# Up projections 512 tokens wide and a seven-product down projection in three banks, in a fused attention and feed-forward kernel

## The chip, the core and the metric

The kernel runs on one core of one Trainium2 chip. The metric is the device time of one execution in microseconds (us). Five instruction queues work side by side: TensorE (PE in the profile, its weight loads PEld), VectorE (DVE), ScalarE (ACT), GpSimd (POOL) and SyncE (SP). They meet only at semaphores.

## What is computed

The reference has two parts. The first is attention with chunk selection, for 4 batches of 8 heads, 768 positions and 64 columns each:

```
ub = sum_d max(q * k_min, q * k_max)          # a bound per query and chunk of 32 keys
top_chunks = the 6 chunks of largest bound, among those not after the query
scores = q @ k.T / 8, kept where the chunk is chosen and the key is not after the query
x = softmax(scores) @ v                       # then [4 * 768, 8 * 64] = [3072, 512]
```

The second is a feed-forward layer over these 3072 tokens, with `w_in` of 512 x 2048 and `w_out` of 2048 x 512:

```
h = max(x @ w_in, 0)
out = (h * h) @ w_out                         # float32, 3072 x 512
```

The kernel takes float32 and multiplies in bf16.

## The kernel before

**Tiles and stages.** Tokens are handled in tiles of 128. The first tile of each batch attends only to itself; these four tiles go through the feed-forward layer together (`x_first`, lines 1401 to 1414). The other five tiles of each batch (640 tokens) follow batch by batch (loop of lines 1451 to 1487): attention writes `x`, `turn` gives its transpose `xT`, `up` makes `h`, and `down` or `down_pair` makes the output rows.

**`up` (line 1203).** One call takes one of 16 blocks of 128 columns of `w_in` and a run of tokens. Four matmuls (line 1214) sum over the 512 input columns in one PSUM bank (`ph`), a ReLU on ScalarE (line 1221) or VectorE (line 1223) writes `ht`, and a square on VectorE (line 413) or ScalarE (line 411) writes into `h2`, the tile that the profile calls `h`. In a batch, tiles 0 and 1 are one run (256 tokens) and tiles 2 to 4 another (384 tokens): two calls for each block (lines 1472 to 1477). An `h2` buffer holds two blocks for all tokens of the batch; there are ten (line 389).

**`down_pair` (line 1236), batches 1 to 3.** Two tiles t and t+1, two halves of the 2048 hidden columns and two halves of the 512 output columns make a 2 x 2 by 2 x 2 block product, done in seven products instead of eight. It needs four combinations of the weights, made once, and sums of blocks of `h`: S1 = upper + lower at t+1, S2 = S1 minus lower at t, S3 = lower at t minus lower at t+1, S4 = upper at t minus S2. Each is made in four pieces 256 elements wide (line 1252). Each product is two parts of four matmuls (line 1288), 256 columns wide, into one half of a PSUM bank:

```
bank 0: P1 | P2    bank 1: P6 | P5    bank 2: P7 | P4    bank 3: P3 | -
```

VectorE adds them up in the output tiles `ob` (`add_up`, line 1325): C11, U2, U4, C22, U3, C21 and C12, each 256 wide, after a copy of P1 to `ob` on either engine. Tile 4 of these batches, and all tiles of batch 0, use `down` (line 1369): four parts of four matmuls, 512 wide (line 1379), then a copy (line 405 or 407). The last batch's tile 4 is cut into 384 and 128 columns. The stores (line 1365) go out on SP, for batches 1 and 2 on POOL.

**What sets the order.** Every operation is entered in a `Plan` (lines 204 to 326) with the engines it may use. `SEQUENCE` (lines 46 to 157) is a written list of all operations by number with a letter for the engine. `Plan.order` gives each a planned start and buffer slots, sorts by start, and `write` issues them in that order on each engine, with matmuls on a constant tile as fillers ahead of early PE operations that are planned to wait (`keep_warm`). Banks in PSUM: three for scores and, in the last batch, the feed-forward layer (`ps`), two for it in the other batches (`ff`), two for the attention sums, one for transposes. The waits are derived from the written order: an operation that writes a bank waits for an operation before it in that order that reads it.

Of the kernel before, what the change touches and what calls it, by code (L numbers as in the profile page):

```python
# [9 lines left out]
F32 = mybir.dt.float32  # L10
# [36 lines left out]
4 61D 6 0 1 131 2 19 8 20 14A 12D 11A 26 5D 21 10D 134 23 135A 9D 22 18 146 7 24 3D  # L47
150 147A 17D 31 136 148 132 25 149D 133A 15D 151 27 176 152 137 177D 28 138 160 142 32
139 140 161A 141 156 33 153 143 174 154 178 155 29 175A 157 179 158 30 144 162 145 180
159 188 184 34 181 163D 190 189A 185 191D 13G 164 182 165 183 35 186 166 187 170 198  # L50
36 192 199D 41 167 171 193A 195 168 172 200A 169 48 196A 286 173 206 197A 194D 204 40
207D 205A 287 280 201 288 54 282A 211 202D 281A 39 212D 208 290D 214 209A 213D 283
215A 217 210A 47 223 284 218A 203A 44 226 219A 285 224A 216D 43 289D 291 227A 343 292
220 225A 293 345A 229 294 295 221A 38 344D 296 230A 232 222D 297A 42 347 235 298A 46
299A 346 313 233A 309 50 228D 314 349 300D 241 236A 45 351 350 310 317 348 301 51 237A
231D 354 234D 238 302 352D 242A 355 334 49 318 353D 250 356 335 62G 60 239A 412 357
322 16 305 251A 414 55 244 358 306 413 323 315G 359 307D 326 243D 247 416A 363D 303G
311D 324G 362D 327 304 52 308 248D 312 330 360A 316 338 331 53 319 253 361D 252D 339
56 415D 364 385 245D 365 368 332G 406 336G 240D 369 325 372 320 328G 256 410 373 370G
59 386 329 409 333 376 254A 380 69 389 377 337 387D 262 411 408D 67 381 321 397 407A  # L60
417 378G 366D 340 257 418 68 398 420 390 367 249D 469 374G 341 246A 401 419 37 393 371
471A 263 421 399G 391D 342 402 422 375 66 379 424D 394 382 388 423D 258 395G 426D 64
383 425A 472 439 435 392 396 436 400 403 470D 427 440 264 255D 428 473 71 431 448 432
259 404 384 65 449 429D 475 452 433G 477 456 73 453 265 437D 476 457 474 57 443 260D
478A 460 480 441D 261 430 70 444 450D 434 481 268 461 482 58 479A 464 483 438 442 445
484 269 72 465 405 266A 485 81 270 486D 462D 78 487D 451 731 488D 498 735 274 458G 499
454G 79 489A 490 446 500D 494 734 491 506 98 455 459 463 495 466 515 732D 271 83 516
733D 507 511 736 496G 467 502 272A 737 74 468 519 512 447 275 82 85 492D 503 738 493
520 739 527 523 513G 741D 497 501 521G 524 742 504D 517G 276 80 740A 743 77 525D 744
505 528 508 794 76 745 514 518 795A 509 522 746 526 529 114 277 530 510 796A 531 94  # L70
747 278A 749D 532 748D 104 533A 534 750D 760 535A 797 584 86 119 585A 539 798 761 764
75 542 540A 768 751D 765 800 541D 578 799 543A 766G 801 777 769 536 90 803D 579A 752
544D 537A 756 802 575 110 753 580D 572 804D 576A 805 762G 573A 577D 545 111 95 538D
757 557 806 546A 574D 857 754G 807 558A 548 758G 547A 87 559D 105 566 859A 549D 781
808 560 100 567A 809 858A 267 581 561D 99 568D 551 562D 782 861 773 582A 755 783G 810
552A 759 91 554 550D 774 812D 763 569 860 583A 775G 789 555A 128 84 767 811A 556D 863
570D 814A 563 862 813A 571D 586 89 867D 770 564A 785 865 587A 776 588 864 778 638 589D
786 779G 1022 88 790 868 96 565D 819 553D 590 866A 771 869 787G 815 820 273 591D 668
92 816 823 870 593 670A 817G 871 780 102 784 594D 831 669A 827 872 788 129 596 124
821D 828 671 639 832 829G 597A 672 836 873 595A 791 108 640 824 877D 598D 837 641 792  # L80
825G 592D 876A 117 673 1021 840 875A 605 874A 772 93 793 674 642A 894 676 878 841 599
675 606A 842D 818 879 106 886 600D 608 895 601D 838G 611 1177A 609D 880G 63G 844 125
607D 822 612A 1117 617 887 882 618A 826 678D 97 830 602 883 613D 610D 620 677A 120
1118 101 833 603A 848 881 884G 1300 621A 890 614 845 1301 622A 126 679 623 891 1176D
107 615A 885 892G 680 899 619A 1119 888G 626 681 900 846G 889 682 103 893 624A 896
901G 903 834 683 122 616A 852 644 835 627A 1179 904 839 121 843 632 625A 1237D 1303
849 684 645 1245D 633A 109 897 850G 1121 628A 1120 907 1302 629 1183A 1178 118 643 646
630A 127 685D 908 905G 1180 635 686D 604A 1304 909G 1124 898 130 688A 116 701 853 1125
647 1238D 687A 1182 1307 1126 702 847 851 689 1127 636A 902 703G 906 1239 697 690 693
650 698 1023 694 699G 911 1240 854 1184A 722 691G 718 695G 651 723 1128 1550 912 1129  # L90
855 910 714 1024 719 652 913G 1308 715 856 112 123 705 648A 710 1181 726 1571 631A 692
720G 696 1244D 700 1185 706 1116D 279 656 1572 711 724G 1309 637A 113 657 1122D 634A
1123D 1310 1132A 712G 914 704 716G 1186 653 1133A 1115D 727 1311 915 1131D 1130A 1167
1312 707 1188 1159 654A 658 708 1187 1160 709 655 659 1168 1161G 1189 916 1306D 1169G
1190 1134 1028 1305A 1138 713 717 1027 917 721 1139 725 728 1163 729 1135 662 918 730
1164 1136G 919 1146 1315A 1155 1547 1165G 920 1171 1140G 1147 663 1156 1316D 1148G
1549 1142 1172 921 1192D 1137 664 1191D 1143 1313D 1194A 1195 1546 1144G 1199 971 660A
115 1150 1141 1193A 1145 1149 1298D 665 1157G 1548 1151 1314D 970 1613 1200 1551 1203
666A 922 1552 1204 1207 972 1026 1152 925 923A 1205G 1612 1208 1158 1211 928 926A 661
1209G 1162 1196 1616 649 1166 1170 1615 1173 1201G 931 929A 1241 927D 924A 1216 1553  # L100
934 932A 1197G 1212 1554 940 1555 935A 1224 933D 1217 1153 937 930D 1614 941A 1228
936D 938A 1556 946 1225 1025 943 1557 947A 1226G 1232 939D 942A 1220 1299D 949 944A
1154 1218G 945A 952 948D 950A 1568 1617 953A 1198 955 1229 951D 1202 967 954A 956D
1230G 1558 1233 1317 1174 968D 964 1221 1175 1206 958 957D 965A 1222G 1618 1329 959A
961 1569 966A 1210 1213 969A 973 962A 1242 1029 960A 1219 976 1243 974A 1214 1040 963A
1619 979 1560 977A 975D 1561 1223 1034 985 980A 1620 1559 1318 1621 982 1562 1570 986A
981D 1573 1035 983A 978D 988 987D 1330 1574 991 989A 1036 1331G 1622 1246 992A 994
990D 1247 984A 1000 1038 995A 1248 993A 1003 1001D 996A 1037 1227 1006 1249 1004A 1250
1002A 1012 1576 1007A 1251 1032 1321 1005A 1593 1009 1030 1013A 1575 667 1010A 1015
1033 1008D 1577 1041 1016A 1578 1042 1011A 1031 997 1579 1591 1045A 1565 1014A 1043  # L110
1564 998A 1252D 1044 1253A 1039 1231 1567 1018 1046 1017A 1215 1566 1255A 1264 1319D
1268 1322 1254D 1047 1590 999A 1580 1048 1323G 1265 1623 1234 1053 1019D 1269 1256
1054 1055 1257 1050 1272 1074 1320 1057 1071 1273 1258G 1056 1285 1270G 1235 1324 1260
1049 1286 1058 1236 1261 1293 1266D 1287G 1061 1059 1583 1020D 1262G 1277 1584 1062
1259 1281 1278 1051 1060 1582 1294 1263 1267 1581 1063 1342 1271 1279D 1274 1343 1068
1075 1064 1052 1275 1289 1282 1338 1276 1344G 1081 1290 1283G 1592 1350 1072 1339 1280
1073 1082 1291D 1563 1069 1325 1284 1076 1065 1326 1078 1077 1083 1351 1066 1333 1327D
1288 1340G 1079 1292 1346 1070 1334 1354 1295 1067 1328 1347 1332 1296 1084 1297 1355
1335 1352G 1097 1348D 1085D 1341 1634 1336 1594 1086 1345 1644 1349 1337 1353 1356
1087 1638 1357 1088 1358 1635 1093 1080 1359 1095 1641 1094 1092 1091 1098 1090 1647  # L120
1089 1360 1096 1099 1642 1657 1645 1104 1648 1101 1410 1105 1636 1651 1100 1106 1654
1637 1102 1595 1107 1411 1643 1109 1103 1596 1108 1639 1361 1597 1660 1586 1362A 1598
1110 1585 1363A 1599 1674 1600 1588 1661 1640 1364 1675 1601 1652 1111 1365A 1662
1366A 1646 1409 1671 1370 1587 1653 1112 1371A 1672 1666 1658 1649 1367 1372A 1667
1602 1677 1368A 1113D 1650 1681 1373 1655 1114 1382 1369D 1678 1374D 1659 1668 1589
1383A 1656 1376 1669 1687 1375D 1379 1384D 1377A 1670 1663 1380A 1682 1424 1684 1378D
# [203 lines left out]
def kernel(  # L330
# [795 lines left out]
    sums = {}  # L1126
# [42 lines left out]
    def ffn(x, ready, rows, by_dma, due, rate, up_tags=("ff", "ff"), by_pool=False):  # L1169
# [33 lines left out]
        def up(f, c0, c1, i):  # L1203
# [4 lines left out]
            if f // 2 not in h2:  # L1208
                h2[f // 2] = buffer("h2", [128, 2, 128 * n])
# [241 lines left out]
    for b in range(B):  # L1451
# [68 lines left out]
```

## Time and profile before

| | us |
|---|---|
| median of 3 runs | 261.51 (261.18 to 262.19) |
| the profiled execution | 261.52 |
| its span in the profile | 259.8 |
| around the span | 1.7 |
| TensorE busy in the span | 245.2 |
| VectorE, ScalarE, GpSimd busy | 219.9, 200.6, 118.0 |

The profiled execution is as long as the median. Busy times are sums over one engine. A matmul row lasts longer than its distance to the next one, since matmuls are pipelined; so a busy TensorE may still issue less than it could, and the distances of starts tell more. `PEld` rows with idle time "issue" are weight loads that did not start although the engine's queue was in their place: the load or its matmul stood at a wait.

### The profile page before, as it was taken

Reading aid. Unit: us, or ns where it says so; the run is one execution under the profiler, and the core shown is the slowest. Engines: PE = TensorE matmul, PEld = TensorE weight load, DVE = VectorE, ACT = ScalarE, POOL = GpSimd, SP = SyncE. Lnnn points to the kernel's source line nnn. Section 1 sums busy time; section 2 is a strip of 40 time slices with the busy share of each in tenths; the row PEclk is TensorE's granted clock in tenths of the full one; section 3 lists DMA queues with packets and bytes.
Section 4 is the critical chain, followed back from the end, with each engine's and each line's share of the span. In section 5 each row is a group of like instructions: output and inputs, shape, how many; then the busy total and the mean of one; then the engine's idle time right before and its main releaser. Section 6 shows DMA issues by size and latency. Waiting matters only on the chain. (4 is left out here: it accounts for less than half of the span.)

```text
span 259.8 us, 7199 instructions
## 1 busy us (share of the span) xinstructions
PE 245.2 (94%) x2633; PEld 174.7 (67%) x2649; DVE 219.9 (85%) x780; ACT 200.6 (77%) x423; POOL 118.0 (45%) x202
## 2 busy tenths in 40 slices
PE   8779999999999999999999998999999999999993
PEld 5556466666687566556687676867776776867773
DVE  5559999989999999999999988888888994578752
ACT  6558999878999999899999896748988961883300
POOL 8999698999985935372411304222022210000000
PEclk9999999999999999999999999999999999999999
DMA  9999999999999999956736529453796025111112
GB/s 131 126 161 190 173 155 193 172 164 141 152 145 188 163 159 131 150 85 104 104 115 144 96 72 187 112 127 84 182 187 106 0 83 101 43 42 44 40 71 91
DMA packets 117283, 31.92 MB, mean 123 GB/s; under 512 B 99840, under 2 KB 114944, under 8 KB 117248
## 3 DMA queue, kind: packets, MB, share of 16 engines
q0 software_dynamic: 77968, 16.00, 72.2%
q1 hardware_dynamic: 39280, 15.47, 30.7%
q8 instruction: 20, 0.33, 0.5%
q14 instruction: 15, 0.12, 0.2%
HBM read 32.77 MB, written 6.55 MB: 151 GB/s over the span
## 5 line engine op out<-in xcount | busy, mean ns | idle before, releaser
L1214 PE MATMUL ph<-xT,w_in_sb 128*128 128x256 bf16 (+2 forms) x592 | 98.8, 304 | 1.1 <-ACT ht L1221 0.2
L1074 ACT ACTIVATE e<-ps 128x512 bf16<-128x512 f32 x120 | 66.8, 603 | 6.6 <-PE ps L1050 5.6
L1214 PEld LDWEIGHTS <-w_in_sb 128*128 128x128 bf16 x592 | 54.5, 97 | 23.7 <-issue 2.8
L1221 ACT ACTIVATE ht<-ph 128x256 bf16<-128x256 f32 (+2 forms) x115 | 51.2, 453 | 16.4 <-PE ph L1214 13.5
L1379 PE MATMUL py<-w_out_sb,h 128*128 128x512 bf16 (+2 forms) x192 | 46.4, 361 | 0.9
L1030 POOL TENSOR_SCALAR_AFFINE_SELECT e<-e 128x128 bf16<-128x128 bf16 (+1 forms) x74 | 26.6, 371 | 43.6 <-ACT e L1074 43.0
L1050 PE MATMUL ps<-kqc 88*128 88x128 bf16 (+1 forms) x240 | 40.3, 272 | 0.4 <-DVE kqc L407 0.2
L411 ACT ACTIVATE h<-ht 128x256 bf16<-128x256 bf16 (+2 forms) x69 | 31.9, 476 | 0.9 <-DVE ht L1223 0.3
L413 DVE TENSOR_TENSOR h<-ht 128x256 bf16<-128x256 bf16 (+2 forms) x79 | 25.7, 335 | 3.3 <-ACT ht L1221 3.0
L1379 PEld LDWEIGHTS <-h 128*128 128x128 bf16 x208 | 18.4, 97 | 14.0 <-issue 0.4
L1365 POOL DMA_DIRECT2D out_dram<-ob x10 | 5.5, 554 | 48.9 <-DVE ob L1325 32.9
L1062 PEld LDWEIGHTS <-e 128*128 128x128 bf16 x480 | 23.4, 97 | 5.6 <-issue 0.2
L1050 PEld LDWEIGHTS <-kqc 88*128 88x128 bf16 x240 | 20.1, 97 | 8.5 <-DVE kqc L407 0.7
L1325 DVE TENSOR_TENSOR ob<-ob,py 128x256 f32<-128x256 f32 x42 | 17.4, 418 | 9.4 <-PE py L1288 8.2
L1145 ACT ACTIVATE e<-ps 128x512 bf16<-128x512 f32 x40 | 21.6, 600 | 3.7 <-PE ps L1107 3.6
L1062 PE MATMUL av<-vn,e 128*128 128x65 bf16 x360 | 23.6, 193 | 0.0
L1223 DVE TENSOR_SCALAR ht<-ph 128x256 bf16<-128x256 f32 (+2 forms) x33 | 16.2, 495 | 6.5 <-PE ph L1214 5.8
L405 ACT COPY ob<-py 128x512 f32<-128x512 f32 (+2 forms) x13 | 6.6, 511 | 19.4 <-PE py L1379 18.8
L1288 PEld LDWEIGHTS <-s 128*128 128x128 bf16 x192 | 18.0, 97 | 5.1 <-issue 2.2
L757 DVE TENSOR_TENSOR x<-av,rc 128x320 bf16<-128x320 f32 (+1 forms) x40 | 18.3, 470 | 0.4
L1030 POOL TENSOR_SCALAR_AFFINE_SELECT mask<-mask 128x256 bf16<-128x256 bf16 x20 | 9.0, 479 | 20.1 <-PE ph L1214 11.9
L1288 PEld LDWEIGHTS <-h 128*128 128x128 bf16 x144 | 13.8, 97 | 5.9 <-issue 3.4
(134 smaller groups left out, 456.4 us busy)
## 6 DMA issues: line engine op xcount, KB each, us to landing
mask<-seen SPq DMA_DIRECT2D x16, 336.0 KB, 7.2
out_dram<-ob SPq DMA_DIRECT2D x13, 256.0 KB, 3.2
out_dram<-ob POOLq DMA_DIRECT2D x10, 256.0 KB, 2.5
w_in_sb<-in_moe_w_in_dram POOLq DMA_DIRECT2D x4, 512.0 KB, 8.3
w_out_sb<-in_moe_w_out_dram POOLq DMA_DIRECT2D x4, 512.0 KB, 8.7
vn<-in_v_dram POOLq DMA_DIRECT2D x15, 128.0 KB, 5.3
nt<-in_k_dram POOLq DMA_DIRECT2D x10, 128.0 KB, 5.5
nt<-in_q_dram POOLq DMA_DIRECT2D x10, 128.0 KB, 6.3
```

Source lines behind the costliest of these rows:

```text
L411: nc.scalar.activation(dst, src, ACT.Square)
L413: nc.vector.tensor_mul(dst, src, src)
L757: return plan.op({"DVE": 0.08 + 0.00108 * D * n}, due, lambda _: nc.vector.tensor_mul(x(), av[:, :, 0:D], rc[:, 0:n].unsqueeze(2).to_broad ...
L1030: nc.gpsimd.affine_select(out=e, in_=e, compare_op=ALU.is_ge, fill=0.0, base=0, channel_multiplier=-1, pattern=[[0, n], [1, 128]])
L1050: nc.tensor.matmul(ps[:, 128 * c:128 * (c + nt)], lhsT=kqs(slice(0, KC), s, hh)[:, 128 * j:128 * (j + 1)], rhs=qss(slice(0, KC), s, hh)[:, ...
L1062: nc.tensor.matmul(av[:, t - 1], lhsT=e[:, 128 * c:128 * (c + 1)], rhs=value_tile(b, h, j), start=(i == 0 and c == 0), stop=(i == len(BANK ...
L1074: nc.scalar.activation(e.tile, ps.tile, ACT.Exp, scale=scale), [sc], [ps, e])
L1145: done = plan.op({"ACT": 0.51}, due + 0.5, lambda _: nc.scalar.activation(e.tile, ps.tile, ACT.Exp, scale=scale), [sc], [ps, e])
L1214: nc.tensor.matmul(ph.tile, lhsT=w_in_sb[:, ki, 128 * f:128 * (f + 1)], rhs=xT[:, c0 // 128:c1 // 128, ki], start=(ki == 0), stop=(ki == N ...
L1221: nc.scalar.activation(ht.tile, ph.tile, ACT.Relu)
L1288: nc.tensor.matmul(bank[:, mid * side:mid * (side + 1)], lhsT=left(f), rhs=right(f), start=(f == 0), stop=(f == half - 1), skip_group_chec ...
L1379: nc.tensor.matmul(py.tile, lhsT=h2[f // 2][:, f % 2, 128 * t:128 * (t + 1)], rhs=w_out_sb[:, f, c0:c1], start=(f == 0), stop=(f == NFI - 1))
```

## The change

Tiles 0 to 3 (512 tokens) become one run of `up`. Tile 4 is done for four blocks together: 16 matmuls of 128 columns into one bank, then one ReLU and one square of 512 elements. An `h2` buffer holds four blocks, and there are five. The sums of blocks are made in two pieces 512 wide. P7 and P4 share one half bank: C22 reads P7, then the matmuls of P4 add onto it (`onto`), so that U3 is left out and C21 is U2 plus that sum; P3 takes the other half, after P4. A pair needs three banks. `SEQUENCE` is written anew for the operations left.

```diff
-    plan = Plan({"tp": 1, "ps": 3, "av": 2, "ff": 2, "e": 8, "h2": 10, "ht": 3,
+    plan = Plan({"tp": 1, "ps": 3, "av": 2, "ff": 2, "e": 8, "h2": 5, "ht": 3,
...
-        def up(f, c0, c1, i):
+        def up(f, c0, c1, i, m=1):
...
-            ph = buffer(tag, [128, w], F32, name="ph")
-            ht = buffer("ht", [128, w])
-            if f // 2 not in h2:
-                h2[f // 2] = buffer("h2", [128, 2, 128 * n])
+            ph = buffer(tag, [128, m, w], F32, name="ph")
+            ht = buffer("ht", [128, m, w])
+            if f // 4 not in h2:
+                h2[f // 4] = buffer("h2", [128, 4, 128 * n])
...
-                for ki in range(NKI):
-                    nc.tensor.matmul(
-                        ph.tile, lhsT=w_in_sb[:, ki, 128 * f:128 * (f + 1)],
+                for k in range(m):
+                    for ki in range(NKI):
+                        nc.tensor.matmul(
+                            ph[:, k], lhsT=w_in_sb[:, ki, 128 * (f + k):128 * (f + k + 1)],
...
-                lambda e: square(e, hs[:, f % 2, c0:c1], ht.tile), [op], [ht, hs],
+                lambda e: square(e, hs[:, f % 4:f % 4 + m, c0:c1], ht.tile), [op], [ht, hs],
...
-                    {"DVE": 0.232}, at[0], go, needs, tiles, port=True)
+                    {"DVE": 0.365}, at[0], lambda _: nc.vector.tensor_tensor(
+                        sums[dst][g].tile, a(), b(), op=op), needs, tiles, port=True)
...
-                                rhs=right(f), start=(f == 0), stop=(f == half - 1),
+                                rhs=right(f), start=(f == 0 and not onto), stop=(f == half - 1),
...
-                     for _ in range(4)]
+                     for _ in range(3)]
...
             p7 = product(banks[2], 0, of_sum(3), mixed(3), *mixed_needs(3, of_s(3)))
-            p4 = product(banks[2], 1, upper(t + 1), mixed(4),
-                         *mixed_needs(4, of_h(half, t + 1)), p7)
             c22 = add_up(corner(1, 1), corner(0, 1), banks[2], 0, [u4, p7], obs)
-            u3 = add_up(corner(1, 0), corner(1, 0), banks[2], 0, [u4, p7], [obs[1]])
-            c21 = add_up(corner(1, 0), corner(1, 0), banks[2], 1, [u3, p4], [obs[1]])
-            p3 = product(banks[3], 0, of_sum(2), w(1, 1), *weights_needs(1, of_s(4)))
-            c12 = add_up(corner(0, 1), corner(0, 1), banks[3], 0, [c22, p3], [obs[0]])
+            p4 = product(banks[2], 0, upper(t + 1), mixed(4),
+                         *mixed_needs(4, of_h(half, t + 1)), c22, True)
+            p3 = product(banks[2], 1, of_sum(2), w(1, 1), *weights_needs(1, of_s(4)), p4)
+            c21 = add_up(corner(1, 0), corner(1, 0), banks[2], 0, [u4, p4], [obs[1]])
+            c12 = add_up(corner(0, 1), corner(0, 1), banks[2], 1, [c22, p3], [obs[0]])
...
-        for c in range(2):
-            tiles = range(2 * c, 2 + (NS - 2) * c)
-            for t in tiles:
-                turn(t)
-            for f in range(NFI):
-                up(f, 128 * tiles[0], 128 * (tiles[-1] + 1), f)
+        for t in range(NS - 1):
+            turn(t)
+        for f in range(NFI):
+            up(f, 0, QC - 128, f)
+        turn(NS - 1)
+        for f in range(0, NFI, 4):
+            up(f, QC - 128, QC, f // 4, 4)
```

More of the change, by code (lines that the diff above doesn't have):

```diff
@@ L1261, in down_pair @@
+            for g in range(2):
+                fs = [*range(4 * g, 4 * g + 4), *range(half + 4 * g, half + 4 * g + 4)]
                 one, two = ([o for f in fs for o in squares_of(f, u)] for u in (t, t + 1))
-                low, high = h2[g], h2[quarters + g]
-                bufs = {s: sums[s][g // 2] for s in sums}
-                add(1, g, 1, lambda g=g: part_of(g, t + 1),
-                    lambda g=g: part_of(quarters + g, t + 1), ALU.add, two,
-                    [low, high, bufs[1]])
@@ L1267, in down_pair @@
-                add(2, g, 2, lambda g=g: piece(1, g), lambda g=g: part_of(g, t),
-                    ALU.subtract, [made_sums[1, g]] + one, [low, bufs[1], bufs[2]])
+                low, high = h2[g], h2[2 + g]
+                add(1, g, 1, lambda g=g: part_of(g, t + 1), lambda g=g: part_of(2 + g, t + 1),
+                    ALU.add, two, [low, high, sums[1][g]])
+                add(2, g, 2, lambda g=g: sums[1][g].tile, lambda g=g: part_of(g, t),
+                    ALU.subtract, [made_sums[1, g]] + one, [low, sums[1][g], sums[2][g]])
@@ L1278, in of_sum, with product @@
             def of_sum(s):
                 return lambda f: sums[s][f // 4][:, f % 4]
-            def product(bank, side, left, right, needs, tiles, before=None):
+            def product(bank, side, left, right, needs, tiles, before=None, onto=False):
                 ops = []
@@ L1386, in down @@
                     [op] + loaded["out", part] + [o for f in fs for o in squares_of(f, t)],
[L1387 removed]
+                    [py, h2[part]])
             op = plan.op({"ACT": 0.057 + w / 1200, "DVE": 0.075 + w / 960}, at[0] + 1,
```

251 lines of the change are left out of this document (116 added, 135 removed).

## The prediction

> **What bounds the kernel now.** I read the page first: the engines' sums and the slices over time.
>
> ```profile
> span 259.8 us, 7199 instructions
> ...
> PE 245.2 (94%) x2633; PEld 174.7 (67%) x2649; DVE 219.9 (85%) x780; ACT 200.6 (77%) x423; POOL 118.0 (45%) x202
> ...
> PE   8779999999999999999999998999999999999993
> ...
> PEclk9999999999999999999999999999999999999999
> ```
>
> TensorE is busy nearly everywhere, at full clock; the dips are at both ends. Then the windows, cut where the stages differ (columns: length, then busy time and count for PE, PEld, DVE, ACT, POOL, the clock, DMA share, GB/s).
>
> ```profile
> 0.00:20.00 20.00, 15.62 (x188) 10.99 (x189) 11.38 (x47) 12.51 (x21) 18.77 (x29) 1.00 1.61 140
> ...
> 30.00:140.00 110.00, 107.72 (x1178) 73.50 (x1189) 105.99 (x368) 103.21 (x215) 74.14 (x126) 1.00 1.54 144
> 140.00:220.00 80.00, 77.19 (x908) 57.19 (x910) 69.10 (x260) 59.71 (x131) 16.47 (x38) 1.00 0.55 115
> 220.00:244.00 24.00, 24.00 (x190) 18.41 (x189) 16.63 (x56) 15.57 (x38) 1.51 (x3) 1.00 0.12 40
> 244.00:259.80 15.80, 11.30 (x99) 8.78 (x96) 7.46 (x23) 0.48 (x2) 0.00 (x0) 1.00 0.22 83
> ```
>
> From 30 to 140 us three engines are full at once; from 140 us on VectorE and ScalarE have room and TensorE alone sets the pace. So the end is moved by what TensorE issues and by its waits, and before 140 us also by work taken from the two others. Now the waits of the seven products, from the list of waits (total us, times, longest) and the timeline:
>
> ```profile
> PEld L1288 <- issue: 5.6, 11, 1.3
> ```
> ```profile
> 168.36 0.60 PE L1288 MATMUL py<-x,s 128*128 128x256 bf16 x4
> ...
> 169.00 0.42 DVE L1325 TENSOR_TENSOR ob<-ob,py 128x256 f32<-128x256 f32 x1 [0.39 <-PE py L1288]
> ...
> 169.47 0.75 PEld L1288 LDWEIGHTS <-s 128*128 128x128 bf16 x7 [0.69 <-issue]
> ```
> ```profile
> 158.39 0.31 PEld L1288 LDWEIGHTS <-h 128*128 128x128 bf16 x3 [1.28 <-issue]
> ```
> ```profile
> 249.23 0.75 PEld L1288 LDWEIGHTS <-h 128*128 128x128 bf16 x7 [0.28 <-issue]
> ...
> 251.65 1.19 PEld L1288 LDWEIGHTS <-s 128*128 128x128 bf16 x11 [0.69 <-issue]
> ...
> 254.07 0.31 PEld L1288 LDWEIGHTS <-h 128*128 128x128 bf16 x3 [0.69 <-issue]
> ```
>
> At 168 us P5 stops between its two parts. VectorE's U2 reads the other half of that bank (P6) and was written ahead of part two, so TensorE waits for it: P5's four matmuls end at 168.96, U2 runs to 169.42, TensorE goes on at 169.47. With no TensorE work between, such a **bank wait costs 0.69 us**; at 158.39, with a queue on VectorE, 1.28. Together 5.6 us in 11 waits.
>
> **The changed matmuls of `up`: nothing.** TensorE gets as many: for 64 blocks, 4 of 256 and 4 of 384 columns become 4 of 512 and 4 of 128, each with its own weight load. The distance of starts is a row's length less one matmul's duration, by the matmuls that follow the first:
>
> ```profile
> 28.57 1.89 PE L1214 MATMUL ph<-xT,w_in_sb 128*128 128x512 bf16 x8 [0.19 <-ACT ht L1221]
> ```
> ```profile
> 245.05 1.46 PE L1379 MATMUL py<-w_out_sb,h 128*128 128x384 bf16 x8
> ...
> 254.50 1.04 PE L1288 MATMUL py<-w_out_sb,s 128*128 128x256 bf16 x8
> ...
> 255.37 1.06 PE L1379 MATMUL py<-w_out_sb,h 128*128 128x128 bf16 x16
> ```
> ```profile
> L1214 PEld LDWEIGHTS <-w_in_sb 128*128 128x128 bf16 x592 | 54.5, 97 | 23.7 <-issue 2.8 <-DMA w_in_sb<-in_moe_w_in_dram 0.6
> L1214 PE MATMUL ph<-xT,w_in_sb 128*128 128x384 bf16 x256 | 49.3, 325 | 0.0
> ...
> L1214 PE MATMUL ph<-xT,w_in_sb 128*128 128x256 bf16 x288 | 39.8, 272 | 0.8 <-ACT xT L405 0.2 <-DVE ht L1223 0.2
> ```
> ```profile
> L1379 PE MATMUL py<-w_out_sb,h x192: 219/379/390, 41.2 to 256.2; 128*128 128x512 bf16 x160, 128*128 128x384 bf16 x16, 128*128 128x128 bf16 x16
> ```
>
> 512: (1.89 - 0.38)/7 = 0.216 us. 384: (1.46 - 0.325)/7 = 0.162. 256: (1.04 - 0.272)/7 = 0.110. 128: (1.06 - 0.22)/15 = 0.056. Before 0.162 + 0.110 = 0.272, after 0.216 + 0.056 = 0.272. The 97 ns of a weight load lie beside other matmuls.
>
> **The bank waits: -4.7.**
>
> ```profile
> 120.63 0.65 PE L1062 MATMUL av<-vn,e 128*128 128x65 bf16 x16
> ```
> ```profile
> L1062 PE MATMUL av<-vn,e 128*128 128x65 bf16 x360 | 23.6, 193 | 0.0
> ```
>
> A value matmul of attention starts (0.65 - 0.193)/15 = 0.030 us after the last. I counted in the order of the changed kernel's TensorE instructions. P4 now must wait until C22 has read P7, in all six pairs. Between P7 and P4 stand, pair by pair: 4 score matmuls (two of 128 and two of 384 columns) and 12 value matmuls (0.11 + 0.32 + 0.36 = 0.79 us), four of 512 columns (0.86), sixteen of 128 (0.90), four of 512 (0.86), and mixtures worth 2.4 and 3.5. All are over 0.69. P3 follows P4 with 1.0 and 1.1 between in two pairs and 0.65 (four of 384) in the last; in the other three it is written ahead of C21, so VectorE waits instead. None of the old bare joints (P5 after U2, P4 after C22, nothing between) is left. I keep 0.9 of the 5.6 us, for a VectorE that comes late: -4.7. Bounds: -5.6, and -1.0 if most come back as lateness.
>
> **Work taken from VectorE and ScalarE: -1.5.**
>
> ```profile
> L1221 ACT ACTIVATE ht<-ph 128x384 bf16<-128x384 f32 x50 | 24.3, 490 | 9.9 <-PE ph L1214 8.8 <-DVE h L413 0.6
> ...
> L1221 ACT ACTIVATE ht<-ph 128x256 bf16<-128x256 f32 x55 | 21.2, 389 | 6.2 <-PE ph L1214 4.4 <-DVE ht L1223 0.5 <-PE ps L1050 0.2
> ...
> L413 DVE TENSOR_TENSOR h<-ht 128x256 bf16<-128x256 bf16 x40 | 11.1, 289 | 1.2 <-ACT ht L1221 1.1
> ...
> L413 DVE TENSOR_TENSOR h<-ht 128x384 bf16<-128x384 bf16 x30 | 10.8, 363 | 2.0 <-ACT ht L1221 1.8
> ...
> L1221 ACT ACTIVATE ht<-ph 128x512 bf16<-128x512 f32 x10 | 5.9, 617 | 0.3 <-PE ph L1214 0.2
> ...
> L413 DVE TENSOR_TENSOR h<-ht 128x512 bf16<-128x512 bf16 x9 | 3.9, 447 | 0.1
> ...
> L1027 DVE TENSOR_TENSOR e<-e,tri 128x128 bf16<-128x128 bf16 x17 | 3.7, 216 | 0.0
> ```
>
> Each block of 640 tokens had two ReLUs (0.389 + 0.490) and two squares (0.289 + 0.363); now it has 1.25 of each: 0.771 and 0.559. That is 0.108 + 0.093 = 0.20 us for 64 blocks, 12.9 us over two engines. The sums of blocks, priced as squares of the same sizes: 16 x 0.289 before, 8 x 0.447 after, 1.0 us for each pair; one `add_up` less, 0.42. From 140 us on this is hidden beside TensorE: nothing. In the full stretch lie some 32 of the blocks, 6.4 us, 3.2 for each engine; but 11 causal masks of 128 go from GpSimd to VectorE (11 x 0.216 = 2.4), and two of 256. So between 0 and -3.2; TensorE is idle there for 110 - 107.7 = 2.3 us by its row. I take half of the ceiling, -1.5.
>
> **The head: +0.7.**
>
> ```profile
> 0.81 0.20 POOL masks.py:197 MEMSET ident<- 128x128 bf16 x1 [0.29 <-POOLq L1504]
> ...
> 1.53 1.04 POOL L505 DMA_DIRECT2D k<-in_k_dram  x1 [0.15 <-issue]
> ```
> ```profile
> 17.83 1.05 PE L1214 MATMUL ph<-xT,w_in_sb 128*128 128x256 bf16 x8
> ```
>
> The first `up` starts at 17.83, when `w_in`'s first quarter has come. In GpSimd's new order 12 loads stand ahead of it, not 9: one of 128 KB and two of 80 KB more, 288 KB at the window's 140 GB/s, 2.1 us. The first load is issued ahead of the identity, some 0.7 us sooner: +1.4. The second quarter is later by 160 KB less the same 0.7, +0.4; the third is not later. Transposes and first-tile values that followed fill part of it. There are 12 more filler matmuls of 128, 12 x 0.056 = 0.7, and I take that; bounds -0.7 and +1.4.
>
> **The tail: +0.4.**
>
> ```profile
> 256.46 0.27 ACT L405 COPY ob<-py 128x128 f32<-128x128 f32 x1 [12.25 <-PE py L1379]
> ```
> ```profile
> out_dram<-ob SPq DMA_DIRECT2D x3, 256.0 KB, 2.0
> ...
> out_dram<-ob SPq DMA_DIRECT2D x1, 64.0 KB, 1.8
> ```
>
> The last matmuls are now P3's, not `down`'s: C12 (0.42) instead of the copy (0.27), and a store of 256 KB (2.0) instead of 64 KB (1.8): +0.35, between 0.2 and 0.8 if three stores queue.
>
> **Sum.** 261.52 (the profiled execution: span 259.8 and 1.7 around it; the median of the runs is 261.51) - 4.7 - 1.5 + 0.7 + 0.4 = **256.4 us**.
>
> **Rivals.** *Given back.* Before 220 us a wait that goes may only uncover the next one, since the attention chain of the last batch runs through VectorE as well; then only the last stage gains (0.28 + 0.69 + 0.69 = 1.66): 261.52 - 1.66 + 0.7 + 0.4 = 261.0. Against it: TensorE is at 96% there, VectorE at 86%.
>
> *Late VectorE (slower).* P4 waits for VectorE's read in six places and P3 in three, most with 0.1 to 0.4 us to spare. If VectorE's queue (masks, sums now 0.45 long) delays each read, TensorE and everything behind it stand. At 0.98 each, the middle of 0.69 and 1.28, nine such waits cost 8.8 us: 261.52 - 5.1 + 8.8 = 265.2. It decides from a mean of 5.1/9 = 0.57 us. For it: the 1.28 at 158.39. Against: four of the nine have 1.0 us or more between.
>
> *Weight loads bound the 128-wide matmuls (slower).* If a load of 97 ns did not overlap, 256 of them would cost 97 - 56 = 41 ns each, +10.5: 266.9. Against it stands the row of sixteen with their own loads in 1.06 us. The Trainium skill, "TensorE: Matmul & The Clock Gate", section "Back-to-back issue gap", gives about 81 ns for each 128-wide matmul in a stream with weight loads; by that figure these would cost 256 x 25 ns = 6.4 us more, an estimate, and the row of 56 ns speaks against it.
>
> *The full stretch follows VectorE.* Then the whole 3.2 us come, and the waits wholly: 261.52 - 5.6 - 3.2 + 0.4 = 253.1.
>
> The Trainium skill's "PSUM — Partial Sum Buffer", section "Terms", says that no two engines may be at one bank at once; the timeline at 168 us agrees. By that rule P4 in P7's place adds no kind of wait that the bank did not have before.
>
> **Chances.** Forecast 0.65, given back 0.14, late VectorE 0.08, weight loads 0.03, full stretch 0.10. Leaving out the two slower rivals and the far side of "given back", the range is 253.0 to 260.8. About 0.5% (1.3 us) is what a measurement can tell from no change: faster 0.74 (forecast and full stretch, less a little), within 0.15, slower 0.11.
>
> **What would show it.** Right: weight loads of the products idle under 1.5 us in all; 128-wide rows of `up` at 56 ns; 140 to 220 us denser on TensorE. Wrong: P4 waiting for C22 in most pairs (late VectorE); the first `up` after 19.5 us; more TensorE idle between 30 and 140 us, where coarser `h2` buffers and half as many bank turns could make ReLUs wait.

## The result and the profile after

The changed kernel takes 259.51 us (median of 14 runs, 257.71 to 263.56; the longest one ran at a disturbed clock and is left out of the ratio), the kernel before 261.66 beside it. The ratio is **0.9911**, 95% interval 0.9888 to 0.9934: faster by 2.3 us, 1.7 to 2.9. The forecast was 256.4, a gain of 5.1: the sign and the range held, the gain is less than half of it.

The page of the changed kernel, its profiled execution taking 259.88 us:

```profile
span 258.2 us, 7044 instructions
...
PE 247.5 (96%) x2661; PEld 167.8 (65%) x2661; DVE 211.2 (82%) x699; ACT 193.9 (75%) x366; POOL 113.4 (44%) x190
...
PE   4989999999989999999999999989999999999994
```

The two helpers have less to do: VectorE by 8.7 us, ScalarE by 6.7. The first slice of TensorE says 4 where it said 8: the head got worse. The windows with the same cuts (PE, PEld, DVE, ACT, POOL, clock, DMA share, GB/s):

```profile
0.00:20.00 20.00, 15.48 (x172) 11.56 (x173) 8.62 (x38) 11.83 (x19) 18.72 (x28) 1.00 1.57 132
...
30.00:140.00 110.00, 108.94 (x1138) 67.80 (x1136) 103.45 (x354) 102.74 (x195) 71.22 (x118) 1.00 1.59 144
140.00:220.00 80.00, 79.21 (x983) 57.62 (x981) 66.39 (x227) 59.30 (x114) 16.19 (x36) 1.00 0.57 117
```

From 140 us on TensorE is denser: 79.21 us of 80 instead of 77.19. The 77.19 and the 107.72 of before are a little low, since that page has 2633 matmuls for 2649 weight loads: 16 matmul records are missing. VectorE has 2.5 us less to do from 30 to 140 us; the experiments will show that TensorE did not get faster by it.

The products' weight loads, by the view of their line (range of durations, then the idle time ahead of them, in us and times):

```profile
L1270 PEld LDWEIGHTS <-s x192: 95/98/100, 156.6 to 254.0; 128*128 128x128 bf16 x192
L1270 PEld LDWEIGHTS <-h x144: 95/98/100, 152.3 to 252.5; 128*128 128x128 bf16 x144
...
  issue: 0.2, 1
```

5.6 us in 11 waits became 0.2 in one. P4 waits for C22 nowhere, so the rival of the late VectorE did not come. Nor did the weight loads bound the 128-wide matmuls of `up`; sixteen of them, each with its own load, in the timeline:

```profile
98.12 1.05 PE L1202 MATMUL ph<-xT,w_in_sb 128*128 128x128 bf16 x16
```

With 0.22 for one, (1.05 - 0.22)/15 = 0.055 us from start to start; 0.056 was forecast. The Trainium skill, "TensorE: Matmul & The Clock Gate", section "Back-to-back issue gap", gives about 81 ns for each such matmul; this trace does not agree.

The tail, from the last matmuls and the last sum:

```profile
253.38 1.03 PE L1270 MATMUL py<-w_out_sb,s 128*128 128x256 bf16 x8
...
254.45 0.42 DVE L1307 TENSOR_TENSOR ob<-ob,py 128x256 f32<-128x256 f32 x1 [1.12 <-PE py L1270]
```

From the start of the last operation on a result to the end of the span it is 258.2 - 254.45 = 3.75 us, and before 259.8 - 256.46 = 3.34: 0.41 longer, +0.4 forecast.

What went wrong is at the other end. The busy time and number of `up`'s matmuls in the first 30 us, before and after (PE, then PEld):

```profile
0.00:30.00 30.00, 9.36 (x55) 5.22 (x56) 1.00 1.63 155
```
```profile
0.00:30.00 30.00, 6.71 (x41) 3.81 (x42) 1.00 1.62 147
```

By 30 us TensorE has done 2.65 us less of `up`. GpSimd's timeline of the changed kernel shows how the head begins, and the timeline of TensorE when the first `up` starts:

```profile
1.34 1.04 POOL L492 DMA_DIRECT2D v<-in_v_dram  x1 [0.83 <-POOLq L1486]
2.38 1.78 POOL L492 DMA_DIRECT2D k<-in_k_dram  x2
4.13 1.08 POOL L492 DMA_DIRECT2D q<-in_q_dram  x1
5.20 0.23 POOL masks.py:197 MEMSET ident<- 128x128 bf16 x1
...
6.28 0.29 POOL L443 TENSOR_SCALAR_AFFINE_SELECT ahead<-ahead 128x128 bf16<-128x128 bf16 x1
6.52 1.00 POOL L492 DMA_DIRECT2D q<-in_q_dram  x1
```
```profile
13.59 0.84 POOL L592 DMA_DIRECT2D w_in_sb<-in_moe_w_in_dram  x1
```
```profile
22.00 1.05 PE L1202 MATMUL ph<-xT,w_in_sb 128*128 128x256 bf16 x8
```

The identity comes at 5.2 instead of 0.8 us, no load is issued between 5.2 and 6.5, `w_in`'s first quarter is issued at 13.59, and the first `up` starts at 22.00 instead of 17.83. The transfer's record in the trace shows when that quarter has landed: at 21.96 us, and before at 17.78; so in both kernels the first `up` starts with it. The prediction named "the first `up` after 19.5 us" as a sign that it is wrong.

### The profile page after: what moved, and what is told of

Its sections match the earlier page's. It is cut to its first block, busy times and chain, and to the rows that moved or that the text cites. A ratio compares the mean times of both kernels' runs of the same rounds, so it can differ in the third digit from the quotient of the medians.

```text
span 258.2 us, 7044 instructions
## 1 busy us (share of the span) xinstructions
PE 247.5 (96%) x2661; PEld 167.8 (65%) x2661; DVE 211.2 (82%) x699; ACT 193.9 (75%) x366; POOL 113.4 (44%) x190
## 4 chain that ended last, share of the span: by engine, by line
PE 85%; ACT 8%; DVE 2%; issue 1%; POOL 1%; POOLq 0%; ACTq 0%
PE ph L1202 33%; PE py L1360 14%; PE py L1270 14%; PE ps L1037 9%; PE av L1049 5%; ACT e L1061 2%; PE T L403 2%; PE av L1127 2%; PE ps L1094 2%; ACT kqc L392 1%; ACT e L729 1%; ACT t L392 1%; PE qT L403 1%; PE kT L403 1%; DVE e L1141 1%
## 5 line engine op out<-in xcount | busy, mean ns | idle before, releaser
L1202 PE MATMUL ph<-xT,w_in_sb 128*128 128x512 bf16 (+2 forms) x592 | 93.0, 304 | 0.4 <-ACT ht L1209 0.2
L1202 PEld LDWEIGHTS <-w_in_sb 128*128 128x128 bf16 x592 | 46.3, 97 | 30.6 <-issue 1.8
L1209 ACT ACTIVATE ht<-ph 128x512 bf16<-128x512 f32 (+1 forms) x80 | 45.2, 577 | 25.8 <-PE ph L1202 20.4
L1017 POOL TENSOR_SCALAR_AFFINE_SELECT e<-e 128x128 bf16<-128x128 bf16 (+1 forms) x61 | 21.8, 372 | 54.0 <-ACT e L1061 53.8
L1360 PEld LDWEIGHTS <-h 128*128 128x128 bf16 x208 | 18.2, 97 | 14.2 <-issue 0.7
L398 ACT ACTIVATE h<-ht 128x512 bf16<-128x512 bf16 (+1 forms) x41 | 24.2, 607 | 2.0 <-DVE ht L1211 1.7
L400 DVE TENSOR_TENSOR h<-ht 128x512 bf16<-128x512 bf16 (+1 forms) x59 | 23.7, 413 | 2.3 <-ACT ht L1209 2.0
L1211 DVE TENSOR_SCALAR ht<-ph 128x512 bf16<-128x512 f32 x20 | 13.7, 689 | 6.5 <-PE ph L1202 4.9
L1141 DVE TENSOR_TENSOR e<-e,mask 128x512 bf16<-128x512 bf16 x40 | 15.9, 437 | 0.4 <-ACT e L1132 0.4
L873 DVE TENSOR_REDUCE kr<-kT 128x24 bf16<-128x768 bf16 x16 | 15.0, 952 | 0.5 <-PE kT L403 0.2
```

Source lines behind the costliest of these rows:

```text
L398: nc.scalar.activation(dst, src, ACT.Square)
L400: nc.vector.tensor_mul(dst, src, src)
L1017: nc.gpsimd.affine_select(out=e, in_=e, compare_op=ALU.is_ge, fill=0.0, base=0, channel_multiplier=-1, pattern=[[0, n], [1, 128]])
L1202: nc.tensor.matmul(ph[:, k], lhsT=w_in_sb[:, ki, 128 * (f + k):128 * (f + k + 1)], rhs=xT[:, c0 // 128:c1 // 128, ki], start=(ki == 0), st ...
L1209: nc.scalar.activation(ht.tile, ph.tile, ACT.Relu)
L1360: nc.tensor.matmul(py.tile, lhsT=h2[f // 4][:, f % 4, 128 * t:128 * (t + 1)], rhs=w_out_sb[:, f, c0:c1], start=(f == 0), stop=(f == NFI - 1))
```

## The experiments

Theory after the result: the bank waits gave what was forecast, and the head took 2.3 us or more of it instead of 0.7, a loss that stays to the end. Rivals: the head's loss is made up in the full stretch, and the gain was missed elsewhere (bank waits given back, or a relief that never came). The operations of the head have the same numbers in both written orders (0 the warm-up memset, 6 the identity, 7 the mask of later keys, 27 `w_in`'s first quarter, 28 the first values of batch 2), so one head can be put on the other body. Every ratio is to the kernel before on the same chip, with its 95% interval; a difference between two experiments is the quotient of their ratios, its interval from the two half-widths by root of squares, times 260 us.

Beside the busy times of `up`, TensorE's work is counted from the traces: each matmul that has started, fillers left out, at the distance of starts of its width (0.025 us for 48 columns, 0.030 for 65, and 0.056 to 0.216 for 128 to 512, as in the prediction). Both kernels have 234.1 us of it in all.

**1. The old head on the changed body** (old_head)

```diff
 SEQUENCE = """
-4 18 28 2 0 22 1 131 19 20 5D 6 17D 7 8 134 21 13A 23 3D 135A 26 12D 132 136 133A 24
+4 61D 6 0 1 131 2 19 8 20 14A 12D 11A 26 5D 21 10D 134 23 135A 9D 22 18 146 7 24 3D
...
```

> The changed kernel with the old kernel's order for everything that is planned before 30 us (loads, identity, transposes, attention of the first tiles, first up blocks; the operations are the same in both kernels), and its own order behind that. Theory (the head lost 2.6 us of TensorE work by 24 to 30 us because the first quarter of w_in lands 4.2 us later, and that loss reaches the end): w_in lands at 17.8 us again, the first up starts there, and the kernel takes 257.0 to 258.0 us, 1.5 to 2.5 less than the changed one. Rival (given back: the full stretch behind it waits for other things, so an earlier head is lost again by 140 us): first up at 17.8 but 259.2 to 259.8 us in all.

257.08 us, ratio **0.9825** (0.9796 to 0.9854): 2.3 us less than the changed kernel, 1.3 to 3.2. The head's work is back:

```profile
0.00:30.00 30.00, 9.04 (x54) 5.07 (x55) 1.00 1.65 155
```
```profile
18.18 1.05 PE L1204 MATMUL ph<-xT,w_in_sb 128*128 128x256 bf16 x8 [1.29 <-DMA w_in_sb<-in_moe_w_in_dram]
```

2.33 us more of `up` by 30 us, 2.3 us less at the end; the theory holds. On the way it is not so even: in all work counted, old_head is 2.4 us ahead of the changed kernel at 30 us, 1.6 at 40, 1.7 at 140 and 2.5 at 240. A third of the loss is made up by 40 us and comes back behind 140; why is not shown.

**2. The new head on the old body** (new_head_on_before): the same exchange the other way round.

```diff
 SEQUENCE = """
-4 61D 6 0 1 131 2 19 8 20 14A 12D 11A 26 5D 21 10D 134 23 135A 9D 22 18 146 7 24 3D
+4 18 28 2 0 22 1 131 19 20 5D 6 17D 7 8 134 21 13A 23 3D 135A 26 12D 132 136 133A 24
...
```

> The kernel before with the changed kernel's order for everything planned before 26 us, its own order behind that. Theory (the head is worth 2 us or more): first up at 22 us, and 263.2 to 264.5 us, 1.5 to 2.8 more than before. Rival (an early loss is made up in the full stretch): 261.3 to 262.2.

266.06 us, ratio 1.0162 (1.0132 to 1.0192): 4.2 us slower, more than the theory said.

```profile
0.00:30.00 30.00, 6.36 (x40) 3.82 (x41) 1.00 1.63 149
```

9.36 - 6.36 = 3.0 us of `up` are missing by 30 us, and 1.2 more are lost behind it. Why it costs more here than on the changed body is not shown. That the head is worth about 2 us or more is shown on both bodies.

**3. The identity first, one load behind `w_in`** (ident_v2). The warm-up memset goes first on VectorE, and the mask of later keys stands behind the eighth load.

```diff
 SEQUENCE = """
-4 18 28 2 0 22 1 131 19 20 5D 6 17D 7 8 134 21 13A 23 3D 135A 26 12D 132 136 133A 24
+4 0 18 6 2 22 1 131 19 20 5D 21 17D 23 8 134 26 13A 7 3D 135A 24 12D 132 136 133A 25
...
```

> The changed kernel with four operations of the head moved and nothing else: the identity first on GpSimd, the warm-up memset first on VectorE, the mask of later keys behind the eighth load, and the load of batch 2's first values behind w_in's first quarter (11 loads ahead of it, not 12). Theory (the queue of load issues on GpSimd sets when w_in lands, 0.87 us each, with 1.3 us of other work between them that left the DMA empty): w_in lands 1 to 2 us sooner, at 20.0 to 21.0, and the kernel takes 0.8 to 1.6 us less than the changed one, 257.9 to 258.7. If the bytes alone set it (128 KB at 140 GB/s): 0.9 us sooner at most and 0.5 us or less in all. Rival (given back): w_in sooner, 259.2 to 259.8 in all.

259.94 us, ratio 0.9928 (0.9901 to 0.9955): against the changed kernel +0.4 us, -0.5 to +1.4. A miss. The first `up` did start at 20.76, as the theory said, and 0.86 us more of `up` was done by 30 us, but no gain can be seen in the time:

```profile
0.00:30.00 30.00, 7.57 (x44) 4.21 (x45) 1.00 1.67 154
```

The first `up` and the row ahead of it:

```profile
20.52 0.40 PE L722 MATMUL av<-v,e 128*128 128x65 bf16 x8 [1.30 <-DMA v<-in_v_dram]
20.76 1.04 PE L1204 MATMUL ph<-xT,w_in_sb 128*128 128x256 bf16 x8
```

By its record in the trace `w_in`'s first quarter has landed at 19.63, 2.3 us sooner than in the changed kernel. TensorE cannot use the last 0.9 of that: it waits for the very load that was put behind `w_in`, the first values of batch 2. So the landing of `w_in` alone is not the whole cause.

**4. The identity late, in the old head** (late_ident). The warm-up memset on VectorE is late again as well.

```diff
 SEQUENCE = """
-4 61D 6 0 1 131 2 19 8 20 14A 12D 11A 26 5D 21 10D 134 23 135A 9D 22 18 146 7 24 3D
+4 61D 18 0 1 131 2 19 20 26 5D 21 6 8 14A 12D 11A 10D 134 23 135A 9D 22 146 7 24 3D
```

> The kernel old_head (the changed kernel with the old head), in which two operations stand late again as in the changed kernel: the identity behind the fourth load on GpSimd, and the warm-up memset on VectorE behind the mask; loads in the old order. Theory A (the order of the loads makes the head's loss, the late identity little): w_in at 18.2 to 18.7, 257.0 to 257.6 us. Theory B (the late identity, which holds up the first transposes and lets TensorE cool down, makes half of it or more): 258.2 to 259.0.

258.45 us, ratio 0.9893 (0.9853 to 0.9934): 1.8 us more than old_head, 0.5 to 3.1. By the time it is theory B, but the trace shows only 0.22 us less of `up` by 30 us, and the first `up` at 18.37, against 18.18 in old_head:

```profile
0.00:30.00 30.00, 8.82 (x53) 4.96 (x54) 1.00 1.64 153
```

Here the time and the head of the one profiled execution do not tell the same; the size stays open.

**5. `w_in`'s first quarter three places later, in the old head** (w_in_13th)

```diff
-... 15D 151 27 176 152 137 177D 28 138 160 142
-32 139 140 161A 141 156 33 153 ...
+... 15D 151 28 176 152 137 177D 32 138 160 142
+33 139 140 161A 141 156 27 153 ...
```

> The kernel old_head (the changed kernel with the old head) with one load moved: w_in's first quarter stands behind three more loads (the first values of batch 2, 128 KB, and two loads of queries, 80 KB each), 12 ahead of it as in the changed kernel, 9 in old_head. Theory A (the place of w_in's first quarter in the queue makes the head's loss): first up at 20.3 to 21.0 us instead of 18.2, 1.5 to 2 us less TensorE work begun by 30 us, and 258.4 to 259.5 us, 1.3 to 2.4 more than old_head. Theory B (it is the order of all loads and of the work that they feed; w_in's place alone is made up by other work): first up late, but under 0.7 us less work begun by 40 us, and 257.0 to 257.8. For the price of a place: if bytes set it, 288 KB at 140 GB/s, 2.1 us later; if the issues on GpSimd set it, 3 x 0.87 = 2.6 us.

258.74 us, ratio 0.9896 (0.9861 to 0.9932): 1.9 us more than old_head, 0.7 to 3.1. The time is theory A's, its mechanism only in part:

```profile
0.00:30.00 30.00, 8.64 (x52) 4.91 (x53) 1.00 1.65 158
```
```profile
19.11 1.04 PE L1204 MATMUL ph<-xT,w_in_sb 128*128 128x256 bf16 x8
```

Three places cost the first `up` 0.93 us, less than the bytes (2.1) or the issues (2.6) say, and 0.4 us of `up` by 30 us. In the changed kernel `w_in`'s first quarter also has 12 loads ahead of it, partly others, and the first `up` starts 2.9 us later still. So by the traces its place is one part among others.

**6 and 7. Loads and work exchanged separately** (loads_only, work_only). loads_only is the changed kernel with all loads, the identity and the mask in the old order; work_only is old_head with these in the new order.

```diff
 SEQUENCE = """
-4 18 28 2 0 22 1 131 19 20 5D 6 17D 7 8 134 21 13A 23 3D 135A 26 12D 132 136 133A 24
+4 18 6 2 0 19 1 131 20 26 5D 21 17D 23 8 134 22 13A 7 3D 135A 24 12D 132 136 133A 31
...
```

> The changed kernel with the 42 loads of GpSimd, the identity and the mask of later keys in the order of the kernel before; every other engine keeps the changed kernel's order. Theory A (the order of the loads alone makes the head's loss): 15.4 us or more of TensorE work begun by 30 us (13.45 in the changed kernel, 15.83 in old_head) and 257.0 to 258.2 us. Theory B (loads and the order of the work that they feed belong together; the new work order on the old loads waits for operands that now come later): 13.5 to 15 us of work by 30 us and 258.8 to 260.5.

```diff
 SEQUENCE = """
-4 61D 6 0 1 131 2 19 8 20 14A 12D 11A 26 5D 21 10D 134 23 135A 9D 22 18 146 7 24 3D
+4 61D 28 0 1 131 2 22 19 20 5D 6 8 14A 12D 11A 10D 134 7 135A 9D 21 18 146 23 26 3D
...
```

> The kernel old_head with the loads of GpSimd, the identity and the mask of later keys in the order of the changed kernel; the other engines keep the old order of the head (four copies of constants behind the identity). Theory A (the loads alone make the loss): as the changed kernel, 13.0 to 14.0 us of TensorE work by 30 us and 259.2 to 260.2 us. Theory B (both belong together): under 13.4 us of work by 30 us and 260 to 262 us, as the old order of work asks for other operands first than the new order of loads brings.

loads_only: 260.86 us, ratio 0.9970 (0.9939 to 1.0000), 1.5 us more than the changed kernel, 0.5 to 2.5. work_only: 264.16 us, ratio 1.0095 (1.0065 to 1.0126), 4.8 more than the changed kernel and 7.1 more than old_head. Both are longer than even theory B said.

```profile
0.00:30.00 30.00, 7.09 (x42) 4.08 (x43) 1.00 1.67 160
```
```profile
0.00:30.00 30.00, 4.71 (x35) 3.37 (x36) 1.00 1.66 152
```
```profile
21.25 1.08 PE L1204 MATMUL ph<-xT,w_in_sb 128*128 128x256 bf16 x8 [0.21 <-ACT xT L394]
```

The third row is loads_only's first `up`: now it is not `w_in`, which has landed at 16.79, that ends the wait but the transposed tile. Before that, until 19.92, TensorE stood for a load of keys (0.73 us by the timeline), which the old order brings later than the new order of work asks for it. Theory B holds in its direction: **the order of the loads and the order of the work that they feed belong together.** Either with the other one is worse than both of one kind, and of the two matching pairs the new one is worse, by 2.3 us on this body.

**8. The old kernel, bank joints filled by hand** (before_order). Eleven operations of TensorE are moved. Here are those at the end, with TensorE's numbers alone (the parts of P5, P7, P4 and P3 are 1945 and 1946, 1949 and 1950, 1951 and 1952, 1956 and 1957; 1967 to 1970 are `down`'s):

```diff
-1945 1946 1949 1950 1951 1952 1956 1957 1967 1968 1969 1970
+1945 1967 1968 1946 1949 1950 1969 1970 1951 1952 1956 1957
```

> The kernel before with eleven TensorE operations moved into six of its bank joints, so that TensorE has 0.4 to 0.9 us of other work while the half of the bank that it is to write next to is read; all operations and shapes as before. Theory (a bank wait costs TensorE its whole length, 4.7 us in these six, and work between takes it away): 257.5 to 259.5 us, 2 to 4 less than before, and under 2 us of idle time ahead of the products' weight loads. Rival (given back: the products that come later make VectorE's sums and what waits for them later, so the wait only moves): 260.5 to 262 us, with the idle time ahead of other lines.

The eleventh operation, meant for the joint of P2, had to stay behind its operand, so five joints were filled. 261.57 us, ratio 1.0008 (0.9979 to 1.0037): no difference, a miss of the theory. Idle time ahead of the products fell only from 5.6 to 4.3 us. One of the joints, at 217 us, shows what happened:

```profile
217.02 0.60 PE L1291 MATMUL py<-x,s 128*128 128x256 bf16 x4
...
217.66 0.42 DVE L1328 TENSOR_TENSOR ob<-ob,py 128x256 f32<-128x256 f32 x1 [0.68 <-PE py L1291]
...
218.14 1.03 PE L1291 MATMUL py<-w_out_sb,s 128*128 128x256 bf16 x8 [0.51 <-DVE ob L1328]
218.14 0.75 PEld L1291 LDWEIGHTS <-s 128*128 128x128 bf16 x7 [0.69 <-issue]
```

The wait of 0.69 us between P5's parts is gone, but U4 (217.66) now stands ahead of P3, and P3 waits 0.69 us for it. There the wait had only moved to the next joint.

**9. The old kernel, its written order searched for joints without work** (before_order2). 18 operations are moved; again TensorE's numbers alone.

```diff
-1934 1939 1935 1936 1940 1945 1946 1949 1950 1951 1952
+1934 1939 1949 1935 1936 1940 1950 1945 1946 1951 1952
...
```

> The kernel before with 18 operations moved within its order behind 145 us (17 of TensorE, one of ScalarE), chosen so that between the two parts that a read of the bank separates TensorE has work; counted in the written order, the joints fall short of 0.69 us by 1.0 us in all, not 5.0 as in the kernel before. Nothing else is changed. Theory (the bank waits cost their length, and order alone takes them away): idle time ahead of the products' weight loads 2 us or less instead of 5.6, and 258.7 to 259.7 us, 2 to 3 less than before. Rival (given back: what is moved ahead makes something else late, as in the first try at such an order): 261.0 to 262.0.

258.82 us, ratio **0.9900** (0.9869 to 0.9932): 2.6 us less than before, 1.8 to 3.4, as the theory said. Idle ahead of the products:

```profile
L1291 PEld LDWEIGHTS <-s x192: 95/98/100, 151.9 to 251.2; 128*128 128x128 bf16 x192
L1291 PEld LDWEIGHTS <-h x144: 95/98/100, 147.9 to 250.4; 128*128 128x128 bf16 x144
...
  issue: 2.2, 4
```

3.4 us of waits less, 2.6 us of time less. Order alone does this, without the wider `up` and the shared half bank.

**10. ReLUs and squares in halves** (halves)

```diff
+            cuts = [(0, w // 2), (w // 2, w)] if w == 512 else [(0, w)]
...
-                    nc.scalar.activation(ht.tile, ph.tile, ACT.Relu)
+                for a, z in cuts:
...
+                        nc.scalar.activation(ht[:, :, a:z], ph[:, :, a:z], ACT.Relu)
```

> The changed kernel, in which each ReLU and each square of 512 columns is issued as two of 256. By the rows of before that is 0.16 us more for a ReLU (2 x 0.389 - 0.617) and 0.13 for a square (2 x 0.289 - 0.447), 0.29 us for each block, somewhat more work for VectorE and ScalarE than the kernel before had. Theory (from 30 to 140 us the two engines limit, so their work is worth half its length there: the term of 1.5 us): with 32 blocks in that stretch, 4.7 us more on each of two engines' mean, 262.0 to 264.2 us. Rival (TensorE sets the pace there as well, the two others have slack, and the relief was worth nothing): 259.2 to 260.3.

261.79 us, ratio 1.0017 (0.9989 to 1.0044): 2.8 us more than the changed kernel, 1.8 to 3.7. It lies between the two theories; the median is below the first one's range and above the second's. VectorE and ScalarE are busy 4.5 and 5.0 us more in all (215.7 and 198.9), but not in the full stretch:

```profile
30.00:140.00 110.00, 107.00 (x1110) 66.76 (x1122) 103.21 (x374) 102.63 (x227) 71.28 (x117) 1.00 1.57 144
140.00:220.00 80.00, 79.76 (x985) 57.74 (x985) 68.84 (x250) 62.52 (x150) 16.43 (x36) 1.00 0.57 117
```

There both are as busy as in the changed kernel (103.45 and 102.74); the surplus turns up behind 140 us. By these rows the two engines have no room from 30 to 140 us, and work that is added to them is paid, some 0.3 us for each us (2.8 of 9.5).

**11. Sums in halves** (sums_halves)

```diff
-                    {"DVE": 0.365}, at[0], lambda _: nc.vector.tensor_tensor(
-                        sums[dst][g].tile, a(), b(), op=op), needs, tiles, port=True)
+                for z in (slice(0, 2), slice(2, 4)):
+                    nc.vector.tensor_tensor(sums[dst][g][:, z], a()[:, z], b()[:, z], op=op)
...
```

> The changed kernel, in which each sum of pairs of 512 columns is issued as two of 256, as in the kernel before: 8 more VectorE instructions for each of six pairs, by the rows of before 16 x 0.289 - 8 x 0.447 = 1.0 us for each pair, 6.3 in all. Theory (from 140 us on VectorE has room beside TensorE, so the wider sums were worth nothing): 259.2 to 260.2 us. Rival (the products and TensorE behind them wait for the sums): 0.3 us or more for each pair, 261.0 to 263.

259.07 us, ratio 0.9910 (0.9883 to 0.9937): no difference from the changed kernel. The wider sums were worth nothing that can be seen, as forecast for work that lies beside TensorE from 140 us on.

**12. old_head with eleven operations behind 30 us moved** (best1). The diff is eleven numbers moved by 2 to 24 places, among them `435`, `853` and `1757`.

> The kernel old_head with eleven operations moved within the order behind 30 us (ten of TensorE, one of ScalarE) so that fewer of them wait for an operand. Expected 256.2 to 257.1 us, 0 to 0.9 less than old_head; if TensorE has no waits left that an order can remove, the same as old_head.

257.82 us, ratio 0.9875 (0.9834 to 0.9916): +1.3 us against old_head, 0.0 to 2.6. A miss: these moves gained nothing. old_head, ratio 0.9825, is the fastest version here.

## Why the prediction was right and wrong

Forecast was a gain of 5.1, measured 2.3. Of the 2.8 that are missing, the head makes 1.6 and the body, waits and relief together, 1.2.

**The head, +0.7: the step that failed.** It measured +2.3 (old_head against the changed kernel), three times as much. What the first `up` waits for was read rightly: it starts when `w_in`'s first quarter has come. The price was wrong. The step took 288 KB at 140 GB/s, 2.1 us, less 0.7 since the first load is issued ahead of the identity, and let other work and fillers halve the rest. The trace has +4.2 us for the first `up`. 3.1 of it is later issue (13.59 against 10.46): three more issues of 0.9 us, and 0.5 us more of GpSimd's own work between loads (from 5.20 to 6.52 it issues none for 1.3 us), while the first load comes only 0.19 us earlier (1.34 against 1.53), since POOL's queue itself starts late. The other 1.1 is a longer way from issue to landing, 8.4 us against 7.3. And the transposes that were to fill the gap stood at the same late identity.

Even the right start of the first `up` would not have given the loss: in experiment 3 it came 1.2 us sooner and no gain was measured, and in loads_only `w_in` came soonest of all and the time was longer. The prediction looked at `w_in`'s loads, where a whole order of loads was exchanged together with the order of the work on the other engines. That the whole exchange costs 2.3 us is shown; how the 2.3 us divide is not. Experiments 4 and 5 put the late identity and `w_in`'s later place into the old head one at a time. By their times (1.8 and 1.9 us, each with about 1.3 to either side) either could make most of the loss; by their traces (0.22 and 0.40 us of `up` by 30 us) neither does.

**Work taken from VectorE and ScalarE, -1.5: also wrong, it came to nothing where it was placed.** before_order differs from the kernel before only behind 145 us, and its page counts 2649 matmuls for 2649 weight loads:

```profile
30.00:140.00 110.00, 108.50 (x1191) 73.65 (x1190) 105.98 (x373) 103.41 (x217) 73.47 (x125) 1.00 1.57 143
```

TensorE is busy 108.50 us there, 108.94 in the changed kernel: 0.4 us, not 1.5. In work counted it does 105.1 us from 30 to 140 us in before_order, 105.1 in the changed kernel and 104.4 in old_head, all three on pages without missing records. So the work that the helpers lost did not let TensorE do more there, and all that the body gained came behind 140 us: old_head is 1.2 us behind before_order at 140 and 2.4 ahead at 240. The idle time of 2.3 us on which the step rested was partly missing records. Yet experiment 10 shows that work added to these engines is not free: taking some away gained nothing that shows, adding some cost 2.8 us.

**The bank waits, -4.7: right in mechanism, near in size.** 5.6 us of waits became 0.2. Order alone took 3.4 us of waits away and gained 2.6 us (experiment 9), 0.76 us for each; 5.4 us of waits would so give 4.1, an estimate from these two rows. All of the body is worth 0.9825, 4.6 us, 5.0 without the tail's 0.4. So the waits gave 4.1 to 5.0; whether the last 0.9 us are waits as well is not shown. Experiment 8 shows why a discount was due: a filled joint can pass its wait on. Together with the relief 6.2 was forecast, 5.0 measured.

**`up`'s matmuls, 0; the sums, hidden; the tail, +0.4: right**, by 0.055 us from start to start, by experiment 11, and by +0.41 in the profiled execution.

**The sum.** -5.0 + 0.4 + 2.3 = -2.3. It closes by its making, since 5.0 and 2.3 both come from old_head. The rivals: *given back* is wrong for the waits as a whole, though 261.0 lay nearer to 259.51 than the forecast, and right for single joints (experiment 8); *late VectorE* and *weight loads* did not occur; *the full stretch follows VectorE* neither, since TensorE was not faster there. The sum of that last rival, 253.1, leaves out the head's +0.7 without saying why; with it it is 253.8.

## What to carry to other kernels

When a written order is replaced, compare the first microseconds as carefully as the part that the change is about: list each load's issue time, count what is computed between the issues, and find for each engine the first operand that it lacks; here a loss at the head was not made up by the end, where the busiest engine was full. Bank waits can be counted in the written order, as joints without work of the writer between two writes that a read separates; filling one joint does not help where the next one is left bare by it. Before a row's idle time is taken as room for a gain, see whether its count of matmuls is complete.

## What the runs showed of the hardware

TensorE begins at half pace, and after a pause in its first microseconds it stayed there longer, while the column of the granted clock shows 1.00. In the kernel before, the first 24 fillers of 128 columns, from 3.39 us on, take 2.05 us; the transposes and the 24 fillers behind them:

```profile
5.28 0.39 PE L416 MATMUL T<-ident,q 128*128 128x128 bf16 x4
5.50 1.50 PE L416 MATMUL T<-ident,warm 128*128 128x128 bf16 x24
```

The same in the changed kernel, after TensorE had waited 1.10 us for the late identity:

```profile
5.84 1.44 PE L403 MATMUL T<-ident,warm 128*128 128x128 bf16 x12 [1.10 <-POOL ident masks.py:199]
7.07 0.63 PE L403 MATMUL T<-ident,q 128*128 128x128 bf16 x4
7.50 3.19 PE L403 MATMUL T<-ident,warm 128*128 128x128 bf16 x28
```

With 0.22 us for one, the starts are (1.50 - 0.22)/23 = 0.056 us apart before and (3.19 - 0.22)/27 = 0.110 after. 28 fillers that would take 1.7 us at the full pace took 3.19 and stood ahead of the next transposes. The length varies: in halves, whose head is the same, the same 28 took 2.39 us. The kernels old_head and late_ident differ only by the late identity and memset: old_head's fillers from 5.23 us on, 24 in 1.50 us, start 0.056 us apart; late_ident's from 7.32 on, 16 in 1.91 us behind a pause of 0.89, start 0.113 apart. The Trainium skill, "TensorE: Matmul & The Clock Gate", section "Wait — 56ns, not 53.3ns?", gives 55.6 and 106.7 ns for a warm and a cold array at 128 columns; both traces agree.

In w_in_13th a load's place in the queue cost less than its bytes or its issues: three places, 288 KB and 2.55 us of later issue (13.03 against 10.48), delayed the first `up` by 0.93 us. The way from issue to landing was shorter instead, 6.0 us against 7.7 by the transfers' records. The runs of one kernel spread by 0.8 us (new_head_on_before, 265.75 to 266.58) to 3.7 (late_ident, 257.19 to 260.92), and loads_only's profiled execution is its shortest; so a trace told the place of a loss here more reliably than its size.
